# Attention outputs transposed by DMA from SP instead of by PE and a PSUM copy

## The chip, the cores and the metric

One core of a Trainium2 chip. The metric is the device time of one execution in microseconds. Runs of one kernel mostly agree within about 1%. A ratio is the mean time of one kernel's fast runs over that of the other's of the same rounds, so it is not quite the ratio of the medians that are quoted beside it.

The engines go by their short names: PE multiplies matrices, ACT, DVE and POOL work on elements, and SP here does nothing but issue transfers to the DMA engines. PSUM is the memory that PE writes. The landing of a transfer is counted from the start of its issue until all its data are there.

## The reference

Polynomial-sketch attention over 4 batches, 4 heads, 1088 tokens of 32 features, followed by a feed-forward layer (FFN) over all 4352 tokens:

```python
def phi(x):                              # x: (4, 4, 1088, 32), S1, S2: (8, 32)
    a = einsum('rd,bhsd->bhsr', S1, x);  b = einsum('rd,bhsd->bhsr', S2, x)
    return outer(a, b)                   # 64 features per token
kv, z = einsum('bhsf,bhsd->bhfd', phi(k), v), phi(k).sum(axis=2)
attn  = einsum('bhsf,bhfd->bhsd', phi(q), kv) / (einsum('bhsf,bhf->bhs', phi(q), z) + 1e-6)
x = attn.transpose(0, 2, 1, 3).reshape(4352, 128)
out = square(relu(x @ w_in)) @ w_out     # w_in: (128, 2048), w_out: (2048, 128)
```

## The kernel before

A small list scheduler in the kernel places some 620 operations on the engines, by a table of priorities (`RANK`) found by a search over the scheduler's own cost estimates, and the program is emitted in that order. PE then keeps to it also where an instruction has to wait: with and without the waits for transposes (runs after and e1_no_wait below) its matmuls stand in the trace in the same sequence, line by line and tile by tile. Attention of the next batch runs beside the FFN of the one before. In the text, batch 1 is `b = 0`.

The attention output of a group of 128-token blocks (`g`: two groups of four and five blocks in batches 2 to 4) is normalized on DVE into `xs`, tokens on partitions. The FFN needs it with features on partitions, in `xT`. So PE transposes each block into PSUM, and ACT or DVE copies the result out:

```python
def f_tx(e, tb=tb, db=db, cols=cols, nx=nx):
    t = at(tb).bitcast(BF16)
    xs = at(db)[2]
    for x in range(nx):
        n = min(128, cols - 128 * x)
        nc.tensor.transpose(t[:, 128 * x : 128 * x + n], xs[0:n, x if nx < 5 else (0, 1, 4, 2, 3)[x], :], ident[0:n, 0:n])
# ...
def f_xe(e, x0=x0, tb=tb, cols=cols):
    fn = nc.scalar.copy if e == "ACT" else nc.vector.tensor_copy
    c0 = S * b + 128 * x0
    fn(xT[:, c0 : c0 + cols], at(tb).bitcast(BF16)[:, 0:cols])
```

The FFN's first matmul reads 512 columns of `xT` at a time:

```python
nc.tensor.matmul(at(hb)[:, step * w : step * w + N], <weights of w_in>, xT[:, n0 : n0 + N], start=True, stop=True)
```

And the input loads of the batch after next wait behind a gate on POOL, a copy that reads the normalized tile of a batch's first group:

```python
if g == 0 and b < B - 1:
    def f_gt(e, db=db):
        nc.gpsimd.tensor_copy(gateb, at(db)[2][:, 0, 0:1])
```

## Time and profile before

| | before |
|---|---|
| median time | 120.84 us (4 runs, 120.46 to 121.15) |
| profiled span, mean granted PE clock | 118.0 us, 0.995 |
| busy PE / DVE / ACT | 92% / 82% / 78% |
| idle of PE before FFN matmuls (L698) | 1.0 us |
| issue of an output store on SP, median | 0.45 us |
| issue to landing of a store, min / median / max | 1.4 / 1.8 / 3.8 us |

In the page's row of slices, each digit is the busy share of one fortieth of the span in tenths, and PEclk is the clock that PE was granted. Before, PE is at 9 nearly throughout:

```profile
PE   5998999999999998999999999999899999999850
...
PEclk9999999999999999999999999999999999999998
```

The issues of output stores on SP (ns min/median/max, first and last start; then us to landing):

```profile
L741 SPq DMA_DIRECT2D out_dram<-osb x50: 315/450/1494, 30.5 to 114.7; - x50
...
DMA to landing us min/median/max: 1.4/1.8/3.8
```

### The profile page before, as it was taken

What the parts mean: (1) busy time and instruction counts of PE and PEld (TensorE: products, weight loads), DVE (VectorE), ACT (ScalarE), POOL (GpSimd) and SP (SyncE); (2) the same over time, 40 slices, a digit from 0 to 9 for tenths busy, and PEclk for the clock granted to TensorE, in tenths of its full rate; (3) what the DMA queues carried; (4) which work ended last, traced back from release to release, by engine and by line L of the source; (5) the groups of instructions that cost most, each with busy time, mean ns of one, the idle gap of its engine ahead of it and who ended that gap; (6) DMA issues with size and microseconds to landing.
All of it is one profiled execution on the core that took longest, in us unless ns stands there. A gap on an engine that the chain in (4) does not pass through costs nothing.

```text
span 118.0 us, 3582 instructions
## 1 busy us (share of the span) xinstructions
PE 108.2 (92%) x1442; PEld 66.6 (56%) x1460; DVE 96.6 (82%) x179; ACT 91.9 (78%) x140; POOL 30.5 (26%) x73
## 2 busy tenths in 40 slices
PE   5998999999999998999999999999899999999850
PEld 2377676665666653555757545447656544567640
DVE  2658579989959699997559999999679989999920
ACT  0542367699885799999997999998649999999910
POOL 6139165593000764600006643300000000000000
PEclk9999999999999999999999999999999999999998
DMA  3960968774210299200401948102200050040522
GB/s 107 291 170 6 154 169 126 105 200 183 37 16 6 62 292 232 73 6 10 74 11 23 298 82 235 24 12 39 48 0 0 3 89 8 6 81 3 89 45 45
DMA packets 22272, 10.19 MB, mean 86 GB/s; under 512 B 19008, under 2 KB 20672, under 8 KB 22256
## 3 DMA queue, kind: packets, MB, share of 16 engines
q0 software_dynamic: 2688, 6.06, 20.6%
q1 hardware_dynamic: 18560, 3.54, 15.1%
q10 hardware_dynamic: 1008, 0.36, 1.4%
q8 instruction: 11, 0.18, 0.7%
q14 instruction: 5, 0.04, 0.1%
HBM read 8.78 MB, written 2.23 MB: 93 GB/s over the span
## 4 chain that ended last, share of the span: by engine, by line
PE 53%; ACT 18%; DVE 12%; issue 8%; DMA 4%; POOL 2%; DVEq 0%; ACTq 0%
PE o L724 16%; PE h L698 15%; ACT r L707 10%; PE h L629 6%; PE o L325 5%; DMA kin<-in_k_dram 4%; DVE g L717 4%; ACT g L715 3%; PE a L538 3%; PE h L583 2%; DVE qp L609 2%; PE a L496 2%; ACT A L598 2%; PE h L496 2%; DVE kT L476 1%
## 5 line engine op out<-in xcount | busy, mean ns | idle before, releaser
L707 ACT ACTIVATE r<-h 128x1024 bf16<-128x1024 f32 x53 | 52.0, 1046 | 4.6 <-PE h L698 3.3
L698 PE MATMUL h<-xT,w_in 128*128 128x512 bf16 (+1 forms) x152 | 36.2, 348 | 1.0 <-ACT r L707 0.7
L724 PE MATMUL o<-g,w_out 128*128 128x512 bf16 (+1 forms) x154 | 33.7, 346 | 1.5 <-DVE osb L731 0.5
L717 DVE TENSOR_TENSOR g<-r 128x1024 bf16<-128x1024 bf16 x46 | 30.6, 698 | 0.7 <-ACT r L707 0.3
L715 ACT ACTIVATE g<-r 128x1024 bf16<-128x1024 bf16 x22 | 23.7, 1089 | 0.2
L698 PEld LDWEIGHTS <-w_in 128*128 128x128 bf16 x160 | 16.6, 115 | 12.6 <-issue 3.1
L724 PEld LDWEIGHTS <-w_out 128*128 128x128 bf16 x160 | 15.1, 98 | 13.4 <-issue 1.6
L709 DVE TENSOR_SCALAR r<-h 128x1024 bf16<-128x1024 f32 x15 | 18.0, 1210 | 1.1 <-PE h L698 1.1
L609 DVE TENSOR_TENSOR qp<-h,A 128x512 f32<-128x512 f32 (+2 forms) x22 | 11.9, 562 | 2.9 <-ACT A L598 2.8
L598 ACT COPY A<-h 128x512 f32<-128x512 f32 (+2 forms) x22 | 10.0, 504 | 4.7 <-PE h L583 4.6
L629 PEld LDWEIGHTS h<-kvz,qp 128*64 128x64 f32 x288 | 9.2, 137 | 3.7 <-DVE qp L609 2.0
L583 PE MATMUL h<-qT,SR 32*64 32x256 f32 (+2 forms) x352 | 10.8, 338 | 0.1
L629 PE MATMUL h<-kvz,qp 128*64 128x66 f32 x288 | 10.4, 225 | 0.4 <-DVE kvz L553 0.2
L325 PE MATMUL o<-wz 128*128 128x512 bf16 x26 | 8.6, 450 | 1.5 <-DVE mk L288 1.2
L538 PEld LDWEIGHTS a<-vp,kp 128*64 128x64 f32 x216 | 6.9, 138 | 2.8 <-issue 2.2
L583 PEld LDWEIGHTS h<-qT,SR 32*64 32x64 f32 x352 | 6.2, 131 | 3.1 <-ACT r L707 0.8
L538 PE MATMUL a<-vp,kp 128*64 128x33 f32 x216 | 7.6, 224 | 0.2
L731 DVE STREAM_TRANSPOSE osb<-o 128x512 f32<-128x512 f32 (+1 forms) x10 | 6.3, 629 | 1.4 <-PE o L724 1.4
L663 POOL COPY gateb<-xs 128x1 bf16<-128x1 bf16 x3 | 0.6, 189 | 25.3 <-DVE xs L652 25.3
L360 POOL DMA_DIRECT2D vin<-in_v_dram x12 | 6.6, 560 | 0.4 <-issue 0.4
L476 DVE STREAM_TRANSPOSE kT<-kin 128x512 f32<-128x512 f32 x8 | 5.3, 681 | 1.4 <-DMA kin<-in_k_dram 1.4
L521 DVE TENSOR_TENSOR kp<-a,ka 128x512 f32<-128x512 f32 (+1 forms) x8 | 5.9, 747 | 0.5 <-ACT kb L511 0.5
(65 smaller groups left out, 88.5 us busy)
## 6 DMA issues: line engine op xcount, KB each, us to landing
kin<-in_k_dram POOLq DMA_DIRECT2D x3, 544.0 KB, 5.1
qin<-in_q_dram POOLq DMA_DIRECT2D x3, 544.0 KB, 3.6
vin<-in_v_dram POOLq DMA_DIRECT2D x12, 128.0 KB, 4.5
out_dram<-osb SPq DMA_DIRECT2D x16, 64.0 KB, 1.9
w_in<-in_moe_w_in_dram POOLq DMA_DIRECT2D x4, 128.0 KB, 3.7
w_out<-in_moe_w_out_dram POOLq DMA_DIRECT2D x4, 128.0 KB, 3.9
qin<-in_q_dram SPq DMA_DIRECT2D x1, 416.0 KB
out_dram<-osb SPq DMA_DIRECT2D x10, 32.0 KB, 1.6
```

The lines of the kernel that those rows point to most:

```text
L325: nc.tensor.matmul(tiles["o"][0][:, 0:512], wz[:, 0:128], wz, start=True, stop=True)
L538: nc.tensor.matmul(t[64 * (h % 2) : 64 * (h % 2) + 64, 33 * (h // 2) : 33 * (h // 2) + 33], kp[i][:, j, h, :], vp[i][:, h, j, :], start=(j ...
L583: nc.tensor.matmul(at(hb[x])[64 * y : 64 * y + 64, c0 : c0 + n], SR[32 * h : 32 * h + 32, ab].rearrange("p x y -> p (x y)"), rhs, start=Tr ...
L598: nc.scalar.copy(at(sA)[:, 0 : 2 * n].rearrange("p (r s) -> p r s", s=n), src(ab=0))
L609: nc.vector.tensor_tensor(out=o, in0=i0, in1=i1, op=ALU.mult)
L629: nc.tensor.matmul(at(nb)[64 * hf : 64 * hf + 64, col(x, pr)], qp[i][:, pr, n0 : n0 + 64], kvz[i][xx % 2][:, pr].rearrange("p y d -> p (y ...
L698: nc.tensor.matmul(at(hb)[:, step * w : step * w + N], w_in[:, 512 * (ct // E) : 512 * (ct // E) + 512].rearrange("p (c e) -> p e c", e=E) ...
L707: nc.scalar.activation(o, view(at(hb)), ACTF.Relu)
L709: nc.vector.tensor_scalar_max(o, view(at(hb)), 0.0)
L715: nc.scalar.activation(at(gb)[:, 0 : W * N], r, ACTF.Square)
L717: nc.vector.tensor_tensor(out=at(gb)[:, 0 : W * N], in0=r, in1=r, op=ALU.mult)
L724: nc.tensor.matmul(at(ob)[:, 0:N], w_out[:, ct, :], at(gb)[:, N * w : N * w + N], start=(ct == 0), stop=(ct == CT - 1))
```

## The change

The intent: take 27 transposes from PE and six copies from ACT and DVE, all three of which are nearly full, and give them to SP and the DMA engines, which have time. Batch 1 keeps PE's transposes. The priorities were searched anew for the new list of operations (`RANK` and `SIDE` replaced, not shown).

```diff
+            if b:
+                for x in range(nx):
+                    n = min(128, cols - 128 * x)
+                    c0 = S * b + 128 * (x0 + x)
+
+                    def f_dt(e, x=x, n=n, c0=c0, db=db, nx=nx):
+                        nc.sync.dma_start(out=xT[:, c0 : c0 + n], in_=at(db)[2][0:n, x if nx < 5 else (0, 1, 4, 2, 3)[x], :], transpose=True)
+                    x_ops.append((c0, c0 + n, add(f"dt{b}.{g}.{x}", {"SP": (0.5, 3.0)}, f_dt, [o_mx], vt(10 + g) + 0.1 * x, uses=[db], dma=0.2)))
+                continue
+
             def f_tx(e, tb=tb, db=db, cols=cols, nx=nx):
```

The pair `(0.5, 3.0)` is what the scheduler believes of the transposes: 0.5 us of SP each; `dma=0.2` is the time for which each keeps the DMA engines busy.

## The prediction

> **What bounds the kernel now.** I read the page's busy table first, then the slices, then busy time by stretch, then the chain of work that ended last, and at the end the waits and the DMA issues. The busy table and the chain by line:
>
> ```profile
> PE 108.2 (92%) x1442; PEld 66.6 (56%) x1460; DVE 96.6 (82%) x179; ACT 91.9 (78%) x140; POOL 30.5 (26%) x73
> ...
> PE o L724 16%; PE h L698 15%; ACT r L707 10%; PE h L629 6%; PE o L325 5%; DMA kin<-in_k_dram 4%; DVE g L717 4%; ACT g L715 3%; PE a L538 3%; PE h L583 2%; DVE qp L609 2%; PE a L496 2%; ACT A L598 2%; PE h L496 2%; DVE kT L476 1%
> ```
>
> PE looks like the bound, but it is not alone. The chain passes through four FFN output matmuls in 0.86 us, 216 ns each, while the mean of the group at L698 is 348 ns: part of PE's busy time is waiting inside matmuls. The stretch from 20 to 106 us, where attention and FFN run side by side, shows all three engines close to full:
>
> ```profile
> 20.00:106.00 86.00, 83.14 (x1065) 49.55 (x1078) 77.03 (x132) 76.88 (x112) 20.74 (x42) 1.00 0.33 78
> ```
>
> The columns are the length, then PE, PEld, DVE, ACT and POOL busy, the clock, the DMA share and GB/s. DVE and ACT are each busy 89% of it. So the middle of the kernel is a loop PE, ACT/DVE, PE over three large PSUM buffers, and work taken from any of the three is worth something, but none of it in full.
>
> A second count of PE: from the end of batch 2's last L629 (40.64 us) to the end of the last batch's (89.46 us) there are 124 matmuls of 512 columns (26.8 us at 216 ns), and at the chain's rates 2.3 us of L629, 2.3 of L538, 2.6 of L583, 1.1 of L496 and 1.0 of transposes: 36 us of matmul at full pace in 48.8 us. Elapsed time is 1.36 times PE's work there. I use that factor below.
>
> The removed step has three groups in the page's lines (one more, for copies out of h, belongs to batch 1, which keeps PE's transposes):
>
> ```profile
> L671 PE MATMUL a<-ident,xs 128*128 128x128 bf16 (+1 forms) x29 | 3.0, 217 | 0.2 <-issue 0.2
> L677 ACT COPY xT<-a 128x576 bf16<-128x576 bf16 (+1 forms) x4 | 2.5, 618 | 0.8 <-PE a L671 0.8
> L677 DVE COPY xT<-a 128x256 bf16<-128x256 bf16 (+2 forms) x3 | 1.2, 388 | 0.6 <-PE a L671 0.6
> ```
>
> On the chain in order of time these steps of batches 2 to 4 stand five times (start, us, what):
>
> ```profile
> 43.93 0.27 ACT xT L677
> ...
> 63.55 0.33 PE a L671 x4
> ...
> 68.38 0.65 ACT xT L677
> ...
> 87.49 0.22 PE a L671 x4
> ...
> 94.34 0.35 PE a L671 x5
> ```
>
> Together 1.82 us: the most that this chain can lose by the removal.
>
> **What the Trainium skill says.** "VectorE: DVE Perf Modes", section "The three transpose paths": a 128x128 bf16 transpose takes 390 ns on TensorE and 1309 ns by the DMA crossbar. The trace has no DMA transpose, so only the first side can be set beside it: 217 ns as recorded, and 55 to 83 ns each on the chain (0.22 and 0.33 us for four), since they are pipelined. "DMA: Bandwidth & Descriptors", section "DMA Transpose (X-bar)": the operation is issued from SP or ACT and takes 2-byte types. The data is bf16 and the issuer is SP, which in this kernel does nothing but issue transfers. Same page, section "Issuing engines are not separate DMA queues": all transfers run on the same 16 engines. The trace agrees: output stores, 1.4 to 3.8 us from issue to landing with a median of 1.8, have a median of 3.0 us between 36 and 52 us, where the next batch's inputs arrive at up to 378 GB/s.
>
> ```profile
> out_dram<-osb SPq DMA_DIRECT2D x4, 64.0 KB, 3.0
> ```
>
> **The change, part by part.** I take the counts from the order of the built programs' instructions.
>
> Removed: 27 PE transposes (9 for each of three batches). At the 69 ns each that the chain's 13 show (0.90 us), 1.9 us of PE. Also six PSUM copies: four on ACT (2.5 us) and two on DVE (0.425 and 0.447 us), 3.3 us.
>
> Moved: the schedule was searched anew, so all engines are reordered. Against before, ACT has 3 more L707 (+3.1), 4 fewer L715 (-4.4), 4 more value copies for the key-value product (0.624 each, +2.5), 2 fewer small ones (-0.6), and its xT copies fall from 3.5 us to about 0.7: -2.1 us in all. DVE has 3 fewer L709 (-3.6), 4 more L717 (+2.8), one more kp product (+0.7), and 0.7 us less of xT copies: -0.8. So ACT and DVE together lose 2.9 us; the other 0.4 of the 3.3 went into taking work from POOL, which has time. Shared over two engines that is 1.45 us of length. PE's 1.9 us over its share of busy is no more than that. The chain's bound is 1.8. I take 1.5 us as the gain if no new wait appears.
>
> Added: 27 transposes on SP's queue. SP's issue of a store took 450 ns in the median; I put a transpose at 0.45 to 1.3 us of SP time, the upper end being the skill's figure, and at 2 us from its issue to landing, like a store. Four in a group then take 2 to 5 us of SP, five 2 to 6.5. All of that is beside other work, unless PE reaches the matmul that reads the columns first. So the question is the slack, from the end of the L629 group that gives a part to PE's first L698 that reads it, in PE's new order:
> - Batch 2: 5.3 us of PE work for the first part, 7.1 for the second; times 1.36, 7 and 9.7 us. Before: 2.6 and 3.7 us of work. The search moved these apart.
> - Batch 3: first part 3.1 us of work (4 and 8 FFN matmuls and 16 of L583), so 4.3 us; second part 4.6, so 6.3 us.
> - Batch 4: first part 3.2, so 4.4 us; second 5.6, so 7.6 us.
>
> From this goes the normalization on DVE: from the end of L629 to the end of xs, 61.67 to 62.91 us in batch 3 before, 1.2 us; for a second part it was 1.5 us in batch 2 and more where DVE was busy, and I take 1.6. Remaining for the transfer: batch 3 first part 3.1 us, batch 4 first part 3.2. Only their first column block is wanted so early, and its transpose stands first in SP's order in both: issue plus 2 us is 2.5 to 3.3 us. That fits or misses by 0.2. Second part of batch 3: its wanted block is third in order, 4.7 us left against 3.4 to 5.9 us. Second part of batch 4: fourth in order, 6.0 us against 3.8 to 7.2. So the expected new waits are 0 to 0.2 us twice and 0 to 1.2 us twice; I take 0.5 us in all.
>
> In front of the transposes of batches 3 and 4 stand eight output stores each (an FFN tile across two batches), 8 x 0.45 = 3.6 us of SP. On DVE there are some 4.7 and 6 us of work between the stores' data and these transposes' data, so the stores should be gone by then, just.
>
> Sum: 120.74 - 1.5 + 0.5 = 119.7. I take off another 0.2 for the end: PE's last run of output matmuls with nothing beside it is 24 of 256 columns now against 32 before, 8 x 0.108 = 0.9 us, most of which ACT and DVE, 55% busy after 106 us, set anyway. That gives 119.5 us.
>
> **Rivals.**
> - The wait takes the place of the work. If a transpose holds SP for well over 1.3 us, or lands after 4 us because the next batch's inputs start at the same moment (POOL's gate for them waits for the same xs), all four late points slip by 1 to 3 us and PE, which runs in order, stands still. For it: the store landing of 3.0 us under load, and the skill's 1309 ns. Against it: the slack in batch 2 is ample, batch 4 has no loads beside it, and input transfers begin a microsecond or more after their gate (gate copy at 38.63 us, traffic from 40.6). It would make 121.5 to 125 us.
> - The removed work was hidden anyway. ACT's copies stand on the chain for 0.92 of their 2.5 us, and the chain closes again over FFN work. Then the time stays at 120.3 to 120.8.
> - The bound falls away more fully: PSUM buffers that the transposes used are free for FFN tiles, so the loop tightens by more than the copies. For it: 348 against 216 ns at L698. Against it: six uses of a small buffer among some 70 of large ones; the a buffer took most. It would make 117.5 to 118.5.
>
> **Range and chances.** Main course 119.5, with 0.8 us either way for the new order; the better rival reaches 117.5, the first 122 before it gets unlikely. The faster verdict needs under 118.3, which takes the full 1.8 us of the chain, no new wait, and some of the tail: 0.2. Slower needs over 123.2, so late points of over a microsecond each: 0.12. Within: 0.68.
>
> **What would show it.** Right: no L671 left for batches 2 to 4; ACT and DVE busy together about 2.9 us less; SP's transposes at 0.45 to 1.3 us each and 2 to 3 us to landing; waits of L698's loads for a transpose under 0.6 us in sum; span about 1.2 us shorter. Wrong: a wait of PE for the xT transposes of over 1.5 us; transposes spaced over 1.5 us on SP; a store or an osb buffer that waits behind them; or ACT and DVE idle more than before by what they lost in work.

## The result, and the profile after

| | before | after |
|---|---|---|
| median time | 120.84 us | 137.46 us (4 runs, 136.96 to 138.64) |
| ratio | | 1.139 (95%: 1.131 to 1.147) |
| span, granted clock | 118.0 us, 0.995 | 135.7 us, 0.962 |
| PE / DVE / ACT busy | 108.2 / 96.6 / 91.9 us | 115.0 / 97.0 / 91.4 us |

The kernel became 14% slower, far outside the range. Executions over 1.5% slower than the fastest of the same kernel are left out of the means. The same two slice rows of the changed kernel:

```profile
PE   6998977998898079999993899999999939999960
...
PEclk9999999999999959999999599999999995999999
```

PE has three holes, and at the end of each the clock falls to half. The chain that ended last, by line, now has the transposes' landing in third place, and SP's issue of them (SPq L671) with 3%:

```profile
PE h L707 12%; PE o L733 11%; DMA xT<-xs 10%; ACT r L716 10%; DMA w_out<-in_moe_w_out_dram 6%; PE a L537 5%; DVE g L726 4%; SPq L671 3%; PE h L582 3%; DMA vin<-in_v_dram 3%; DVE qp L608 3%; PE h L628 3%; DMA w_in<-in_moe_w_in_dram 3%; DMA kin<-in_k_dram 2%; DVE xs L651 1%
```

PE's own instructions in order of time show the holes (start, us, engine, line, operation, count, and in brackets the idle time before and what ended it). L707 is the FFN's first matmul:

```profile
48.23 2.72 PE L707 MATMUL h<-xT,w_in 128*128 128x512 bf16 x6 [4.66 <-DMA xT<-xs]
...
75.22 1.04 PE L707 MATMUL h<-xT,w_in 128*128 128x512 bf16 x2 [2.98 <-DMA xT<-xs]
...
112.03 0.71 PE L707 MATMUL h<-xT,w_in 128*128 128x512 bf16 x2 [2.34 <-DMA xT<-xs]
```

Ten microseconds of direct waiting, one hole per batch. The first line shows the second cost too: six matmuls took 2.72 us where six took 1.29 us on the chain of before. The busy times by stretch around the first hole (length, then PE, PEld, DVE, ACT, POOL busy, clock, DMA share, GB/s) put the half clock at its end and behind it, some 3.4 us in all:

```profile
45.00:48.00 3.00, 0.00 (x0) 0.00 (x0) 1.30 (x4) 0.27 (x1) 0.56 (x1) 0.93 0.72 138
48.00:50.00 2.00, 1.77 (x5) 0.69 (x6) 0.00 (x0) 0.71 (x1) 0.57 (x2) 0.50 0.58 189
50.00:52.00 2.00, 2.00 (x22) 0.86 (x21) 1.01 (x1) 1.16 (x4) 0.00 (x0) 0.75 0.05 8
```

What the transposes themselves did: the line's own view, for batch 2, batch 3's first group, and all of batch 4 (ns min/median/max of SP's time for an issue, first and last start; then the time from the start of an issue to landing):

```profile
L671 SPq DMA_TRANSPOSE xT<-xs x9: 1176/1231/2596, 38.0 to 49.6; - x9
...
DMA to landing us min/median/max: 2.3/3.9/7.2
```

```profile
L671 SPq DMA_TRANSPOSE xT<-xs x4: 1095/1230/1230, 69.7 to 73.4; - x4
...
DMA to landing us min/median/max: 5.3/5.5/6.3
```

```profile
L671 SPq DMA_TRANSPOSE xT<-xs x9: 1095/1227/1231, 100.8 to 110.9; - x9
...
DMA to landing us min/median/max: 2.3/2.4/2.9
```

Two things are to be seen. Each block costs SP 1.23 us, one after the other, 2.7 times a store. And landing takes 2.3 us where no input loads run (batch 4), but 5.3 to 7.2 us in the first groups of batches 2 and 3, where the input loads run. The two arrive together because the gate of those loads reads the same tile as the transposes.

So the holes differ. In batch 2 PE wanted blocks 0 and 1, but SP issued block 3 first: the third issue began at 41.87 us and landed 6.23 us later, at 48.10. In batch 3 the wanted block was the very first issue, and it alone took 5.44 us. In batch 4 no loads run, but the wanted block was the fourth of its group: issued at 109.63, landed 2.36 us later. (The order of the blocks on SP is that of the program.)

### The profile page after: what moved, and what is told of

The parts are those of the page before. It is cut to its first block, busy times and chain, and to the rows that moved or that the text cites. A ratio compares the mean times of both kernels' runs of the same rounds, so it can differ in the third digit from the quotient of the medians.

```text
span 135.7 us, 3585 instructions
## 1 busy us (share of the span) xinstructions
PE 115.0 (85%) x1433; PEld 66.2 (49%) x1433; DVE 97.0 (72%) x179; ACT 91.4 (67%) x137; POOL 27.3 (20%) x70
## 4 chain that ended last, share of the span: by engine, by line
PE 35%; DMA 24%; DVE 13%; ACT 12%; issue 6%; SPq 3%; POOL 2%; DVEq 0%; POOLq 0%; ACTq 0%
PE h L707 12%; PE o L733 11%; DMA xT<-xs 10%; ACT r L716 10%; DMA w_out<-in_moe_w_out_dram 6%; PE a L537 5%; DVE g L726 4%; SPq L671 3%; PE h L582 3%; DMA vin<-in_v_dram 3%; DVE qp L608 3%; PE h L628 3%; DMA w_in<-in_moe_w_in_dram 3%; DMA kin<-in_k_dram 2%; DVE xs L651 1%
## 5 line engine op out<-in xcount | busy, mean ns | idle before, releaser
L716 ACT ACTIVATE r<-h 128x1024 bf16<-128x1024 f32 x56 | 54.9, 1032 | 21.0 <-PE h L707 19.5
L707 PE MATMUL h<-xT,w_in 128*128 128x512 bf16 (+1 forms) x160 | 40.3, 369 | 12.4 <-DMA xT<-xs 10.0
L726 DVE TENSOR_TENSOR g<-r 128x1024 bf16<-128x1024 bf16 x50 | 33.9, 696 | 8.2 <-ACT r L716 5.6
L733 PE MATMUL o<-g,w_out 128*128 128x512 bf16 (+1 forms) x160 | 37.8, 362 | 1.3 <-DVE osb L740 0.8
L707 PEld LDWEIGHTS <-w_in 128*128 128x128 bf16 x160 | 17.1, 118 | 28.6 <-DMA xT<-xs 12.0
L718 DVE TENSOR_SCALAR r<-h 128x1024 bf16<-128x1024 f32 x12 | 14.5, 1216 | 7.5 <-PE h L707 7.5
L724 ACT ACTIVATE g<-r 128x1024 bf16<-128x1024 bf16 x18 | 19.0, 1061 | 0.8 <-PE o L733 0.5
L628 PE MATMUL h<-kvz,qp 128*64 128x66 f32 x288 | 10.4, 224 | 1.8 <-DVE qp L608 0.6
L628 PEld LDWEIGHTS h<-kvz,qp 128*64 128x64 f32 x288 | 9.2, 137 | 5.2 <-DVE kvz L552 1.5
L324 PE MATMUL o<-wz 128*128 128x512 bf16 x30 | 10.2, 474 | 1.2 <-DVE wz L319 1.2
L520 DVE TENSOR_TENSOR kp<-a,ka 128x512 f32<-128x512 f32 (+1 forms) x9 | 6.5, 745 | 1.6 <-PE a L495 1.0
L520 POOL TENSOR_TENSOR kp<-kb,ka 128x512 f32<-128x512 f32 x3 | 3.2, 1069 | 19.7 <-ACT kb L510 19.7
```

The lines of the kernel that those rows point to most:

```text
L324: nc.tensor.matmul(tiles["o"][0][:, 0:512], wz[:, 0:128], wz, start=True, stop=True)
L628: nc.tensor.matmul(at(nb)[64 * hf : 64 * hf + 64, col(x, pr)], qp[i][:, pr, n0 : n0 + 64], kvz[i][xx % 2][:, pr].rearrange("p y d -> p (y ...
L707: nc.tensor.matmul(at(hb)[:, step * w : step * w + N], w_in[:, 512 * (ct // E) : 512 * (ct // E) + 512].rearrange("p (c e) -> p e c", e=E) ...
L716: nc.scalar.activation(o, view(at(hb)), ACTF.Relu)
L718: nc.vector.tensor_scalar_max(o, view(at(hb)), 0.0)
L724: nc.scalar.activation(at(gb)[:, 0 : W * N], r, ACTF.Square)
```

## The experiments

Theory after seeing the result: PE's in-order wait for a transpose makes the hole, by (a) landing beside loads and (b) SP's serial 1.23 us per block; each hole also costs PE half its clock for a while (c). Rivals: the new order of all engines (d), and the transposes' own traffic and SP time (e). All experiments:

| run | order | transposes of batches 2 to 4 | median us | ratio to before |
|---|---|---|---|---|
| after | new | DMA, 27 | 137.46 | 1.139 |
| e1_no_wait | new | DMA, 27, not waited for | 124.46 | 1.028 |
| e11_none_after | new | none | 123.10 | 1.018 |
| e3_no_loads | new | DMA, 27, no loads beside | 127.57 | 1.058 |
| e4_wide | new | DMA, 9 | 129.62 | 1.066 |
| e7_wide_early | new | DMA, 9, loads earlier | 122.82 | 1.020 |
| e9_filler | new | DMA, 27, PE kept busy | 132.44 | 1.097 |
| e5_before_order | before's | DMA, 27 | 132.65 | 1.102 |
| e6_none | before's | none | 119.53 | 0.992 |
| e8_hybrid | before's | DMA for two groups, loads earlier | 121.00 | 1.005 |
| e10_hybrid2 | before's | as e8, issued earlier | 120.78 | 0.999 |
| e12_before_wide | before's | DMA, 9, loads earlier | 121.34 | 1.006 |
| e13_early_only | before's | PE, loads earlier | 120.69 | 0.997 |

The kernel before stood at 120.4 to 120.9 us beside them.

### e1_no_wait: nobody waits for the transposes (wrong result)

```diff
-                        xT[:, n0 : n0 + N], start=True, stop=True)
+                        xT[:, n0 : n0 + N] if n0 + N <= S else xT[:, 256 : 256 + N], start=True, stop=True)
```

> The changed kernel, same instructions in the same order, but the first FFN matmul of batches 2 to 4 reads columns of batch 1, so that nobody waits for the DMA transposes (wrong result on purpose). My theory: the waits of PE for transposes (10 us direct in the changed kernel's trace) and the half-speed clock after each of them (some 3 to 4 us) go, about 13.5 us; what remains over the kernel before, 2 to 4 us, is the new order, above all at the start. Expected 122 to 126 us. Rival, waits are only a symptom and the new order or SP's traffic is the cause: 130 us or more. Rival, the new order costs nothing: under 120 us.

124.46 us, ratio 1.028 (1.022 to 1.033), granted clock 1.0. As the theory said: waits and what follows from them are 1.139 - 1.028 = 11.1% of 120.8 us, 13.4 us (give or take 1 us, by the two intervals), and some 3 us over before remain for another cause.

### e11_none_after and e6_none: the order by itself (wrong results on purpose)

e11 is e1 with the issue of the transposes left out too. e6 is the kernel before with transposes and copies of batches 2 to 4 left out and the FFN on batch 1's columns as in e1.

```diff
 # e6_none, in f_tx and in f_xe
+                if b:
+                    return
```

> The kernel before in its own order, with the transposes of batches 2 to 4 and their six copies left out altogether and nothing in their place; the FFN reads batch 1's columns for the later batches (wrong result on purpose). This is the most that any other way of transposing could win in this order. My prediction put it at 1.5 us, bounded by the 1.8 us on the chain: expected 118.2 to 119.5 us. Rival, the removed work was hidden: 120 us or more. Rival, it frees more than itself since nobody waits for the normalized tile either: under 118 us.

> The changed kernel's order with no transposes at all for batches 2 to 4, by PE or by DMA, and the FFN on batch 1's columns (wrong result on purpose); the counterpart of the run of before's order without transposes (119.5 us). Theory that the 124.5 us of the run in which nobody waited were the new order's, not the transposes' traffic: 123.5 to 125 us, so 4 to 5 us for the order alone. Rival, the traffic and SP's queue cost it: 119 to 121 us.

e6: 119.53 us, ratio 0.992 (0.988 to 0.996). So in before's order, transposes that cost nothing at all would win 0.8%, 1.0 us: less than the 1.5 us that I predicted. e11: 123.10 us, ratio 1.018 (1.013 to 1.023), a smaller loss than I expected. Both have no transposes, so 1.018 - 0.992 = 2.6%, 3.1 us, is the new order's. That goes for the order (d). e1 lies 1.0% above e11, so the transposes' traffic and SP time (e) may cost about 1.2 us even when nobody waits; but the two intervals, half a percent each way, overlap, so this last figure is not shown clear of noise.

Where the order loses is not shown. FFN tile 1 is finished (its output transposed on DVE) at 46.68 us in e11 against 43.29 in e6, but tile 3 is level again (69.97 against 70.43), and only from tile 4 (81.81 against 77.67) does e11 stay some 4 us behind to the end.

### e3_no_loads: landing without the loads (wrong result)

```diff
-            nc.gpsimd.dma_start(out=dst, in_=src)
+            if not skip:                  # skip: k, v and q of batches 3 and 4
+                nc.gpsimd.dma_start(out=dst, in_=src)
```

> The changed kernel without the input loads of batches 3 and 4 (their buffers keep the inputs of batches 1 and 2; wrong result on purpose), transposes as they are. Theory that the input loads, released by the same normalized tile as the transposes, stretch the transposes' landing: landing of all transposes falls to 2.2 to 2.5 us (from 5.3 to 7.2 for batches 2 and 3), PE's wait in batch 2 falls from 4.7 to under 1.2 us, in batch 3 from 3.0 to under 0.5, time 126 to 131 us. Rival, SP's issue of 1.23 us each is what PE waits for: waits stay over 2.5 us in each batch, time 134 us or more.

127.57 us, ratio 1.058. Landing fell to 2.2 / 2.3 / 3.3 us, and PE's idle before the transposes' readers to 0.39 us in batch 2 and 0.52 in batch 3. Cause (a) is shown for these two (e7 below shows it again, with correct results). In batch 4 the wait is what it was, as it must be if that one is (b):

```profile
43.86 1.46 PE L708 MATMUL h<-xT,w_in 128*128 128x512 bf16 x6 [0.39 <-DMA xT<-xs]
67.08 0.41 PE L708 MATMUL h<-xT,w_in 128*128 128x512 bf16 x1 [0.52 <-DMA xT<-xs]
102.40 0.81 PE L708 MATMUL h<-xT,w_in 128*128 128x512 bf16 x2 [2.34 <-DMA xT<-xs]
```

### e4_wide: four blocks in one transpose

`xs` got a sixth slot, and its blocks were laid out so that a group's four lie side by side. The transposes stay in the same place in the order.

```diff
-    nc.sync.dma_start(out=xT[:, c0 : c0 + n], in_=at(db)[2][0:n, <block>, :], transpose=True)
+    nc.sync.dma_start(
+        out=xT[:, c0 : c0 + n * w].rearrange("p (x n) -> p x n", n=n),
+        in_=at(db)[2][0:n, y : y + w, :].rearrange("p x c -> p (x c)"), transpose=True)   # w = 4, or 1 for the last 64 tokens
```

> The changed kernel with the four full blocks of a group in one DMA transpose (9 instead of 27 in all), in the same place in the order. Theory that an issue's cost is mostly fixed (64 rows took 1.10 us of SP, 128 rows 1.23): a wide one takes 1.5 to 2.2 us of SP, batch 4's wait of 2.3 us goes, the waits of batches 2 and 3, which come from landing beside the loads, stay at 2 to 5 us each: 131 to 135 us. Rival, the cost is per block: a wide one takes 4 to 5 us, time 137 us as before.

129.62 us (127.95 to 131.18; the ratio rests on two runs), correct. Better than expected: SP's time hardly depends on the size at all, four blocks take what one took, and the wait of batch 2, which I expected to stay, nearly went. The expectation's "64 rows took 1.10 us" was a misreading. By the program's order the three 64-row transposes of the changed kernel took 1.24, 1.09 and 1.23 us; the other two near 1.09 were first in their groups, with 128 rows.

```profile
L678 SPq DMA_TRANSPOSE xT<-xs x9: 1118/1199/1954, 37.6 to 101.7; - x9
DMA to landing us min/median/max: 2.3/2.8/6.3
```

The wait of batch 4 is gone. In batch 2 0.77 us are left, which end with a result of ACT that comes 0.04 us after the transpose has landed. In batch 3, where the first transpose still meets the loads (5.9 us to landing), PE still waits 3.58 us. So (b) is shown as well, for batch 4 and for the wrong order of blocks in batch 2: it was the number of instructions, not the data.

### e7_wide_early: the loads out of the way

```diff
-                    nc.gpsimd.tensor_copy(gateb, at(db)[2][:, 0, 0:1])
+                    nc.gpsimd.tensor_copy(gateb, kp[i][:, NJ - 1, H - 1, F - 1 : F])
```

> The one-transpose-per-four-blocks kernel of the earlier run (129.6 us), with the input loads of batches 3 and 4 released by the key products instead of the normalized tile, so that most of them are through before the transposes. Theory that what is left of the waits there (3.6 and 1.3 us in batch 3) is landing beside loads: landing of all transposes 2.2 to 3 us, no wait of PE for one over 0.8 us, 123 to 126 us, that is, the time of the run in which nobody waits (124.5). Rival, loads are not the cause or the earlier loads disturb other work: 128 us or more.

122.82 us, ratio 1.020 (1.016 to 1.023), correct, a shade under the expected range. Landing 2.3 / 2.4 / 3.3 us; the longest wait of PE for a transpose is 0.4 us. It ends at the time of e11, which has no transposes: with these two edits nothing of the DMA way is left to see in this order, only the order itself.

### e9_filler: PE kept busy in the holes

```diff
+    FILL = {(2, 2): 18, (4, 2): 11, (7, 2): 8}      # (FFN tile, step): matmuls on zeros
             def f_m1(e, m=m, hb=hb):
+                for _ in range(FILL.get((n, m), 0)):
+                    nc.tensor.matmul(at(hb)[:, 0:512], wz[:, 0:128], wz, start=True, stop=True)
```

> The changed kernel with matmuls on zeros (18, 11 and 8 of 512 columns; 3.9, 2.4 and 1.7 us) put in front of the three FFN matmuls at which PE waits longest for a transpose; they need less time than PE waits there. Theory that each wait is followed by a stretch at half clock, which costs 3 to 4 us in all: granted clock 0.99 or more, 133.5 to 135.5 us. Rival, the lower clock lies where PE had time anyway: 136.5 us or more.

132.44 us, ratio 1.097 (1.092 to 1.103): 37 useless matmuls make the kernel 4.2%, 5.0 us, faster, more than I expected. The clock was 1.0 (the profiled run is the slowest of the four, 133.99 us). The size fits the changed kernel's granted clock: 0.962 over 135.7 us is 5.2 us of full-speed time that PE was not given. Cause (c) is shown, and it is a good third of the 13.4 us. How long a hole must be for it is not shown: in e3, where the 2.34 us before batch 4's reader is the one hole over 1 us left after the start in the profiled run, the mean clock was 0.986 in two of the four runs and 1.0 in the other two.

### e5_before_order and e12_before_wide: the DMA way in before's order

e5 puts one transpose per block where PE's stood. e12 issues wide ones right behind the normalization, with e7's gate.

```diff
 # e5_before_order, in f_tx (f_xe returns at once for b > 0)
+                if b:
+                    for x in range(nx):
+                        <n, c0 as in the change>
+                        nc.sync.dma_start(out=xT[:, c0 : c0 + n], in_=<block x of xs>, transpose=True)
+                    return
 # e12_before_wide, at the end of the normalization f_den
+                for y, w in ((0, 4), (4, 1))[: nx - 3] if by_dma else ():
+                    n, c0 = (64 if y else 128), S * b + 128 * (x0 + y)
+                    nc.sync.dma_start(<as in e4_wide>, transpose=True)
```

> The kernel before in its own order, with one DMA transpose per block from SP in the place where PE's transposes of batches 2 to 4 stood, and no copies for them. Theory, the latency is more than any slack in the order: before's order has 2.6 and 3.7 us of PE work as slack in batch 2 and 2.2 in batch 3, less than the changed kernel's, so the waits are longer, 4 to 7 us in each batch, less the start's 2 to 4 us: 134 to 145 us. Rival, the searched order of the changed kernel is what went wrong: under 128 us.

> The kernel before in its own order with all transposes of batches 2 to 4 by DMA, four blocks in one, issued right after the normalization, and the next loads released by the key products: the change with its two dearest faults mended and without the new order. From the end of the normalization to landing it takes 1.2 plus 2.4 us; before's order leaves about 2.0 us in both parts of batch 2, 1.7 in the first part of batch 3 and 2.5 in that of batch 4. Theory: waits of PE of 1 to 2 us in each of these, 4 to 6 us in all, less the 0.85 that the work is worth: 122 to 125.5 us. Rival, the waits are absorbed: under 121 us.

e5: 132.65 us, ratio 1.102. I expected 134 to 145: with less slack its waits (9.3 us) are no longer than the changed kernel's, since there too most of a wait is landing beside loads, which slack of a microsecond or two does not cover. The rival (under 128) is out as well. e12: 121.34 us, ratio 1.006 (1.002 to 1.010), below my 122 to 125.5. My expectation there added SP's 1.2 us to 2.4 us of landing, but the profile counts landing from the start of the issue: 2.4 us is all of it. The waits left are small, 0.55 us before a reader in batch 2, and 0.97 in batch 3 that the profile puts down to the normalization but that ends as the transpose issued at 63.85 us lands.

So the same idea, in before's order, with a third of the instructions and without the loads beside it, costs 0.6% where the change cost 13.9%.

### e8_hybrid, e10_hybrid2 and e13_early_only: is there a version that wins?

Only the second groups of batches 3 and 4 go by DMA, where before's order has most slack; PE keeps the rest. e8 issues in the place of PE's transposes, e10 right behind the normalization, and e13 is the control with e7's gate alone.

```diff
 # e8_hybrid, in f_tx; e10_hybrid2: by_dma = b > 1 and g == 1 in e12's loop
+                if b > 1 and g:
+                    <two wide transposes>
+                    return
 # e13_early_only: e7's edit of the gate, in the kernel before
```

> The kernel before in its own order; PE keeps the transposes of every first part and of batch 2, and only the second parts of batches 3 and 4, which have over 6 us of PE work as slack, go by DMA (two transposes each, four blocks and one), with the next loads released by the key products. Removes 10 PE transposes and two copies (0.65 us of ACT, 0.45 of DVE). Theory that a DMA transpose costs nothing where the slack is over SP's 1.2 us plus 2.3 us of landing: 119.7 to 120.6 us, no wait of PE for a transpose. Rival, even these waits show: over 121 us.

> As the hybrid run before (121.0 us), but SP issues the two transposes of the second parts of batches 3 and 4 right after the normalization in the order, so that in batch 4 they do not stand behind four output stores, which held them from some 92 to 94.8 us there. Theory: the last wait of PE for a transpose (0.7 us) goes, 119.8 to 120.6 us against 120.4, at most a third of the 0.85 us that free transposes of all groups won. Rival, moving work to DMA costs elsewhere as well: 121 us again.

> A control for the runs with earlier loads: the kernel before, PE transposes and all, with nothing changed but that the input loads of batches 3 and 4 are released by the key products instead of the normalized tile. Theory that this alone neither gains nor costs here, so that what the run of before's order with wide transposes shows (121.3 us, 0.6% over before) is the transposes' own: 120.2 to 121.0 us, same. Rival, the earlier loads gain by themselves and hid a cost of the transposes: under 120 us. Rival, they cost: over 121.2 us.

e8: 121.00 us, 1.005 (1.002 to 1.009), above what I expected; in batch 4 `xs` was done at 91.88 us, but SP stood before two output stores (not four, as e10's expectation says) whose data came at 93.72, issued the first transpose at 94.78, and PE waited 0.66 us. e10: 120.78 us, 0.999 (0.995 to 1.004); that wait is gone, and the kernel is level with before. e13: 120.69 us, 0.997 (0.992 to 1.001): the gate alone changes nothing that can be told from noise. None beats the kernel before; with e6's ceiling of 0.8% for all six groups, two groups could not have shown much.

## Why the prediction was wrong

By its own steps:

- **The gain, "I take 1.5 us".** Right in kind, too large: e6 puts it at 1.0 us. One argument under it was weak: I read the mean of 348 ns at L698 as waiting inside matmuls, since they follow each other at 216 ns. The Trainium skill, "TensorE: Matmul & The Clock Gate", section "Single matmul latency", gives (398 + N) / 2.4 for a warm matmul, an estimate of 379 ns at N = 512, and the trace's median is 379 (the mean mixes 104 matmuls of 512 columns with 48 of 256): it is the latency of one matmul in a pipeline, no sign of waiting. A sign that I had named failed as well: ACT and DVE together were busy 188.4 us against 188.5, not 2.9 us less (187.4 in e11, where nothing waits for transposes); why is open.
- **"0.45 to 1.3 us of SP time" per transpose.** Held, at the upper end: 1.23 us.
- **"At 2 us from its issue to landing, like a store".** This is the step that failed. It holds without loads (2.3 us with SP's time in it), but in the first groups of batches 2 and 3 it was 5.3 to 7.2. I had the warning in hand, stores at 3.0 us under load, and the rival named the loads that start with the same tile; I set them aside with "input transfers begin a microsecond or more after their gate". They do, but a transpose that is still in flight when they begin is caught. That rival was right in kind but put at 121.5 to 125 us: slips of 1 to 3 us each, and nothing for the clock or the new order.
- **"The slack in batch 2 is ample".** PE reached the reader at about 43.5 us, 6.9 us after the end of the last L628 of the part, just as worked out (7 us). But I checked the place of the wanted block in SP's order for batches 3 and 4 and not for batch 2, where block 3 is issued first. With landing at 6 to 7 us it made the longest wait of the three.
- **"Second part of batch 4: fourth in order, 6.0 us against 3.8 to 7.2".** Here the transfer was within its range and the slack was too large: the block landed 6.7 us after `xs` was done (105.31 to 111.98), and PE stood before the reader after 4.4 us (at 109.69), not 6.0. That is the third hole, 2.3 of the 10 us.
- **"The expected new waits ... I take 0.5 us in all".** 10 us direct, 11.1% or 13.4 us with what follows.
- **Not in the prediction at all: the clock.** With each of the three holes of 2.3 to 4.7 us PE's clock was at half for some 3.4 us, from about the hole's end on; that costs 5.0 us in all (e9).
- **"With 0.8 us either way for the new order".** The order costs 3.1 us (e11 against e6). The search had looked for a better order with the scheduler's own costs; on the chip it is the worse one even where transposes are free. Why is open.

The sum, as shares of before: -0.8% for the work removed, +2.6% for the order, +1.0% for traffic and SP (not clear of noise), +11.1% for waits and clock: 13.9%, by construction. Within the waits, taking away the loads wins 8.1% (e3) and taking away two thirds of the instructions 7.3% (e4); they overlap: in batch 2 a block that lands late and a block that is issued late meet in the same hole.

## What to carry to other kernels

Here a DMA transpose cost its issuer by the instruction, not by the byte (1.20 us for four blocks, 1.23 for one): give it as many blocks as its form takes, and put the block that is wanted first at the head. Before a synchronous step on a full engine is replaced by a DMA, look at what else is released by the event that releases it, and take its landing time from a transfer of this kernel under that load. And count a hole in PE for more than its length, since the clock can fall with it, as it did here with holes of 2.3 to 4.7 us.

## What the Trainium skill lacked or had wrong

- "DMA: Bandwidth & Descriptors", section "DMA Transpose (X-bar)", gives no cost of an issue (a table in the page's part on trn3 has counts of cycles for earlier generations, none for SBUF to SBUF at this size). Here a transpose held SP 1.23 us in the median, for 128x128 and for 64 rows alike, and 1.20 us in the median of e4_wide's nine, where a plain store took 0.45. That four 128-column blocks in one instruction take no more of SP than one is on none of the pages that I read.
- "VectorE: DVE Perf Modes", section "The three transpose paths": 1309 ns for a 128x128 bf16 transpose by DMA. As SP's time per instruction this is near (1.23 us), but from issue to landing it is 2.3 us unloaded and up to 7.2 us beside loads, and four blocks cost no more SP time than one.
- "DMA: Bandwidth & Descriptors", section "Rules for kernel authors", says a transpose next to ordinary DMAs "needs nothing". That is about correct results, and it held in all runs with right inputs; what the page lacks is the cost in time: landing 5.3 to 7.2 us against 2.3.
- "TensorE: Matmul & The Clock Gate", section "What's actually happening", puts the fall of the clock after an idle window of about 3.4 us. In the changed kernel's profiled run it fell with every hole, also those of 2.34 and 2.98 us; in e3, whose profiled run has a hole of 2.34 us left, two of the four runs kept a mean clock of 1.0.
